# Issuing GpSimd's stores from ScalarE in an attention-plus-MLP backward kernel

## The chip, the cores and the metric

The kernel runs on one core of a Trainium2 chip. Its time is the device time of one execution in microseconds (us). A core has five engines with an instruction queue each: TensorE (PE, matmuls), VectorE (DVE), ScalarE (ACT), GpSimd (Pool) and SyncE (SP, which here only starts transfers). Transfers (DMAs) are started by an instruction in one of these queues and then carried by 16 DMA engines that all queues share. An engine takes its instructions in the order of its queue; where one waits, those behind it wait too.

## The reference

One decoding step of a transformer layer, with the gradients of everything. The inputs are one row x of 640 numbers, the caches K and V (32 heads of 8192 rows by 128), the weights wq, wo, w1, w3, w2, and the gradient of the output.

```python
xn  = layernorm(x)
q   = xn @ wq                                   # 32 heads of 128
p   = softmax(q . K * 128**-0.5)                # per head, over 8192 rows
out = x + (p @ V) @ wo + (silu(xn @ w1) * (xn @ w3)) @ w2
# outputs: out, and by the vjp of grad_out: dx, dK, dV, dwq, dwo, dw1, dw3, dw2
```

For a head, with do the gradient that comes back through wo: dV = p (outer) do; dp = V . do; ds = p * (dp - sum(p * dp)); dK = ds (outer) q; dq = ds @ K. All large arrays are bf16. Each of K, V, dK and dV is 2 MB a head, so a head reads 4 MB and writes 4 MB, and 303.69 MB move in all.

## The kernel before

**A head.** The 8192 rows of a head lie as 128 partitions by 64 rows. K and V of a head are loaded whole by SP (`load_k` L109 into 3 buffers, `load_v` L115 into 2). The products with q and do are made in two halves: VectorE multiplies (`T`, L347, 4 a head) and TensorE adds up the product's columns in PSUM by eight matmuls with the identity (L349, into `psS` for K and `psDP` for V). Then come small steps: the row maximum (`mrow` L382, a matmul to spread it L384, `negM` L389), the exponentials with their sum on ScalarE (`E`, `rsum`, L392), that sum over all partitions on TensorE (L393, called RSUM in what follows), its reciprocal `rZ` on VectorE (L397), the probabilities (`P2` L399, `Pf` on ScalarE L401), `row_dots` (L414 to L418, rdot on TensorE), `U` (L422), and two sets of 64 narrow matmuls that give the head's output and dq (L407, called PV, and L429, called UK).

**The outer products.** dV and dK of a head are made in two halves each, in one of 4 buffers `ot`: in each half ScalarE makes 8 of 32 rows (L362), VectorE the other 24 (L369). When the second half is made, the 2 MB tile is stored by an issue on Pool (L376, 60 tiles). The last two heads are stored in halves by SP (L374).

**The loop.** The loop over heads (L631 to L679) is pipelined by hand: while head c is finished (probabilities, outer products), the products of head n = c + 1 are made between. The loop calls, in this order: product S of n, first half; `probs`; `outer` dV half 0; `keep_dq` of the head before (L465, ScalarE copies `ps_db`); `row_dots`; `attend` (PV); product S, second half; `outer` dV half 1; `dscores` (`U`, `Uf`, UK); `outer` dK half 0; `keep_wq` (wqT, L439); `row_max` of n; product DP, first half; `outer` dK half 1; `exps` of n (negM, E, RSUM); product DP, second half; `weights` (`odq` L444, `dq_diag` L448, `om` L452, and on TensorE db L450, om L455, dxn L458).

**Groups.** Heads go in groups of four (`GH`). Between the steps, at calls of `gap()`, pieces of two generators are put in. `prep_steps` prepares the next group in the group's third and fourth heads: q of four heads (`ps_q`, L257, five matmuls on the loaded `wq_g`), transposes of wo (`ps_t`, L247, called pst4: four matmuls each, copied to `woT` by ScalarE, L252) and do (`ps_d`, L269, called psd; `do_g` L278). `finish_steps` runs in the first head of the next group, the finish head: the sum `on` (L287, L289), 20 matmuls into `accbank` with `wo_g` (L292, called on20), then ScalarE turns `wo_g` in place into dwo (L301, four rows), stores it with `store()` (L126, on Pool) and makes dwq in place of wq (L308, five rows), which is stored after every second group. Stores marked late are kept in a list and issued in head H - 3.

**The start.** The MLP's gradients are made while the first heads load: dw2 in three parts, stored at L558 and L560, dw1 at L589, dw3 at L600, all issued on Pool.

**What sets the order.** The queues of VectorE, ScalarE, SP and Pool keep the order in which the program is written:

```python
with tc.manual_schedule(engines=ORDERED):
```

TensorE is not in `ORDERED`. The framework's scheduler places its matmuls among each other; only PV's first matmul and some at the start are pinned by `tc.keep_in_program_order`.

Of the kernel before, what the change touches and what calls it, by code (L numbers as in the profile page):

```python
# [16 lines left out]
P = 128  # L17
# [4 lines left out]
def kernel(  # L22
# [22 lines left out]
    nc = tc.nc  # L45
# [4 lines left out]
    F = B_w1.shape[1]  # L50
# [10 lines left out]
    NF, REST = divmod(F, P)  # L61
# [31 lines left out]
    dw1_v = out_6.rearrange("(p ci) f -> p ci f", ci=NC)  # L93
    dw3_v = out_7.rearrange("(p ci) f -> p ci f", ci=NC)
    w2_v = B_w2[0:NF * P, :].rearrange("(b p) c -> p b c", p=P)
    dw2_v = out_8[0:NF * P, :].rearrange("(b p) c -> p b c", p=P)

    with tc.manual_schedule(engines=ORDERED):
# [14 lines left out]
        def load_v(h):  # L113
            Vt = (kpool if h == 1 else vpool).tile([P, J, DH], BF16, name="Vt", tag="K" if h == 1 else "V")
            nc.sync.dma_start(Vt[:], vc[h])  # L115
            kv_tiles[h] = kv_tiles.get(h, [None, None])
            kv_tiles[h][1] = Vt
# [4 lines left out]
        def store(dst, src, later=False):  # L122
            if later:
                late.append((dst, src))
            else:
                nc.gpsimd.dma_start(dst, src)  # L126


        def load_wq(b):
# [12 lines left out]
        w1t = kpool.tile([P, NC, F], BF16, name="w1t", tag="K")  # L142
        w3t = kpool.tile([P, NC, F], BF16, name="w3t", tag="K")
        nc.sync.dma_start(w1t[:], w1_v)
        w2_parts = []
        for b0 in range(0, NB, 6):
            nb = min(6, NB - b0)
            nfull = min(nb, NF - b0)
            w2c = opool.tile([P, nb, D], BF16, name="w2c", tag="o")
# [183 lines left out]
        def product(st, which, half):  # L333
            if which == "S":
                st.q = st.G["qs"][:, st.hh, :]
                src, vec = st.K, st.q
            else:
                st.do = st.G["do"][:, st.hh, :]
                src, vec = st.V, st.do
            if half == 0:  # L340
                st.ps = getattr(st, "ps", {})
                st.ps[which] = ps_acc.tile([P, J, RUN], F32, name="ps" + which, tag="acc")
            ps = st.ps[which]
            DHH = DH // 2
            ds_ = slice(half * DHH, (half + 1) * DHH)
            T = tpool.tile([P, J, DHH], BF16, name="T", tag="T")
            nc.vector.tensor_tensor(T[:], src[:, :, ds_], vec[:, ds_].unsqueeze(1).to_broadcast([P, J, DHH]), ALU.mult)  # L347
            for i in range(DHH // RUN):
                nc.tensor.matmul(ps[:], lhsT=ident_bf[:], rhs=T[:, :, RUN * i:RUN * (i + 1)],  # L349
                                 start=(half == 0 and i == 0), stop=(half == 1 and i == DHH // RUN - 1))  # L350

        def outer(st, vec, w2, wf, dst, h, half):
            outer_v(st, vec, w2, dst, h, half, outer_s(st, vec, wf, half))

        def outer_s(st, vec, wf, half):
            if half == 0:
                st.ot = opool.tile([P, J, DH // 2, 2], BF16, name="ot", tag="o")
            j1 = (half + 1) * JH
            if wf is None:
                return j1  # L360
            for j in range(ACT_J):
                nc.scalar.activation(st.ot[:, j1 - ACT_J + j].rearrange("p a b -> p (a b)"), vec, ACTF.Copy,  # L362
                                     scale=wf[:, half, j:j + 1])
            return j1 - ACT_J

        def outer_v(st, vec, w2, dst, h, half, j1):
            j0 = half * JH
            n = j1 - j0
            nc.vector.tensor_tensor(st.ot[:, j0:j1],  # L369
                                    vec.rearrange("p (a b) -> p a b", b=2).unsqueeze(1).to_broadcast([P, n, DH // 2, 2]),  # L370
                                    w2[:, j0:j1, :].unsqueeze(2).to_broadcast([P, n, DH // 2, 2]), ALU.mult)
            rows = st.ot[:].rearrange("p j a b -> p j (a b)")
            if h >= H - TAIL:
                nc.sync.dma_start(dst[h][:, j0:j0 + JH, :], rows[:, j0:j0 + JH, :])  # L374
            elif half:
                nc.gpsimd.dma_start(dst[h], rows)  # L376

        def row_max(st):
            st.S = small.tile([P, J], F32, name="S_sb", bufs=1)
# [7 lines left out]
        def exps(st):  # L387
            negM = small.tile([P, 1], F32, name="negM")
            nc.vector.tensor_reduce(negM[:], st.sm[:, 8:8 + P], AX.X, ALU.max, negate=True)  # L389
            st.E = small.tile([P, J], F32, name="E", bufs=1)  # L390
            rsum = small.tile([P, 1], F32, name="rsum")
            nc.scalar.activation(st.E[:], st.S[:], ACTF.Exp, bias=negM[:], scale=1.0, accum_out=rsum[:])  # L392
            nc.tensor.matmul(st.sm[:, 3:4], lhsT=ones_f, rhs=rsum[:], start=True, stop=True, skip_group_check=True)  # L393
# [26 lines left out]
        def dscores(st):  # L420
            st.U2 = small.tile([P, J, 2], BF16, name="U2", bufs=1)
            nc.vector.scalar_tensor_tensor(st.U2[:], st.DP[:].unsqueeze(2).to_broadcast([P, J, 2]), st.sm[:, 4:5], st.P2[:],  # L422
                                           ALU.subtract, ALU.mult)
            st.Uf = None
            if st.h < H - 1:
                st.Uf = small.tile([P, 2, ACT_J], F32, name="Uf")
                nc.vector.tensor_copy(st.Uf[:], st.U2[:, :, 0].rearrange("p (a j) -> p a j", a=2)[:, :, JH - ACT_J:JH])  # L427
            for j in range(J):
                nc.tensor.matmul(st.ob[:, 1:2], lhsT=st.K[:, j, :], rhs=st.U2[:, j, 0:1], start=(j == 0), stop=(j == J - 1),  # L429
                                 skip_group_check=True)  # L430
# [39 lines left out]
        def mlp_steps():  # L470
# [55 lines left out]
            for wi in range(2):  # L526
# [4 lines left out]
                for k, b0 in enumerate(range(0, NB, 4)):  # L531
# [6 lines left out]
                    src = bc_ps[:].rearrange("p b a -> p (b a)")[:, 0:cols]  # L538
# [10 lines left out]
            def w2_grad(k):  # L549
                b0, nb, nfull, w2c = w2_parts[k]  # L550
                for b, rows in blocks[b0:b0 + nb]:
                    for ci in range(NC):
                        nc.tensor.matmul(accbank[:, OUT0 + ci:OUT0 + ci + 1], lhsT=w2c[0:rows, b - b0, ci * P:(ci + 1) * P],
                                         rhs=hcol_bf[0:rows, b:b + 1], start=False, stop=True, skip_group_check=True)
                    nc.scalar.activation(w2c[0:rows, b - b0, :], g_bc_bf[0:rows, :], ACTF.Copy, scale=hcol[0:rows, b:b + 1])
                    if b in (1, 3, 5, 7, 9):
                        yield
                nc.gpsimd.dma_start(dw2_v[:, b0:b0 + nfull, :], w2c[:, 0:nfull, :])  # L558
                if nfull < nb:
                    nc.gpsimd.dma_start(out_8[NF * P:F, :], w2c[0:REST, nfull, :])  # L560

            dx_ps = ps_w.tile([P, NC, DR1], F32, name="dx_ps", tag="w")

# [22 lines left out]
            grad_v(0, w1t, 0, 2)  # L586
            dx_part(0, w1t, 4, 1)
            grad_v(0, w1t, 2, 3)
            nc.gpsimd.dma_start(dw1_v, w1t[:])  # L589
            load_v(1)  # L590
            yield from w2_grad(1)
            dx_part(1, w3t, 0, 2)
# [4 lines left out]
            grad_s(1, w3t, 0, 4)  # L597
            yield
            grad_v(1, w3t, 4, 1)
            nc.gpsimd.dma_start(dw3_v, w3t[:])  # L600
            load_k(2)
            yield
            nc.vector.tensor_reduce(dxn_mlp[:], dx_ps[:], AX.X, ALU.add)
# [27 lines left out]
        for h in range(H - 1):  # L631
            n = new_head(h + 1) if h + 1 < H else None
            c = hs.pop(h)
            g, hh = divmod(h, GH)
            if n:
                product(n, "S", 0)
            probs(c)
            outer(c, c.do, c.P2, c.Pf, dvc, h, 0)
            if prev:
                keep_dq(prev)  # L640
            gap()
            row_dots(c)
            attend(c)
            turn_wq(c)
            if n:
                product(n, "S", 1)
            outer(c, c.do, c.P2, c.Pf, dvc, h, 1)
            if h + 2 < H:
                load_v(h + 2)
            gap()  # L650
            dscores(c)
            outer(c, c.q, c.U2, c.Uf, dkc, h, 0)
            keep_wq(c)
            if n:
                row_max(n)
                product(n, "DP", 0)
            outer(c, c.q, c.U2, c.Uf, dkc, h, 1)
            if h + 3 < H:
                load_k(h + 3)
            if h == H - 3:  # L660
                for dst, src in late:
                    store(dst, src)
            gap()
            if n:
                exps(n)
                product(n, "DP", 1)
            weights(c)
            gap()
            if hh == 0 and g + 1 < NG:
                if (g + 1) % HB == 0 and g + 1 > HB:  # L670
                    load_wq((g + 1) // HB)
                if g:
                    load_wo(g + 1)
            if hh == 1 and g + 1 < NG:
                steps.append(prep_steps(g + 1))
                gap()
            if hh == 2:
                gap()
            prev = c  # L679
# [85 lines left out]
```

## Time and profile before

| what | us |
| --- | --- |
| time, median of 3 runs (737.46 to 739.82) | 738.92 |
| span of the profiled execution, first to last instruction | 739.3 |
| VectorE busy | 627.9 |
| TensorE busy | 550.8 |
| ScalarE busy | 469.0 |
| Pool busy | 45.7 |

The profile gives one execution. Its span is 0.4 us above the median of the runs. Instructions are grouped by line and by the tiles that they write and read, `out<-in`; "idle before" is the time that the engine stood still just ahead of them, with what ended it. A view of waits sums that time by engine and releaser. The page cuts the span into 40 slices of 18.5 us and gives the busy share of each engine in tenths. Mean durations that the steps use: T 2.28 us, a VectorE outer product of 24 rows 1.75, a ScalarE row 0.389, eight psS matmuls at full TensorE clock 1.89, a store of 2 MB 19.4 us from its issue to its landing, a load of K 25.4. The mean granted TensorE clock is 0.771.

Of the 303.69 MB, 160.39 MB went by the queue of the hardware's descriptors (SP's transfers), 142.30 MB by the software queue (Pool's).

### The profile page before, as it was taken

What the parts mean: (1) busy time and instruction counts of PE and PEld (TensorE: products, weight loads), DVE (VectorE), ACT (ScalarE), POOL (GpSimd) and SP (SyncE); (2) the same over time, 40 slices, a digit from 0 to 9 for tenths busy, and PEclk for the clock granted to TensorE, in tenths of its full rate; (3) what the DMA queues carried; (4) which work ended last, traced back from release to release, by engine and by line L of the source; (5) the groups of instructions that cost most, each with busy time, mean ns of one, the idle gap of its engine ahead of it and who ended that gap; (6) DMA issues with size and microseconds to landing.
All of it is one profiled execution on the core that took longest, in us unless ns stands there. A gap on an engine that the chain in (4) does not pass through costs nothing.

```text
span 739.3 us, 15756 instructions
## 1 busy us (share of the span) xinstructions
PE 550.8 (75%) x6497; PEld 323.2 (44%) x6513; DVE 627.9 (85%) x708; ACT 469.0 (63%) x1395; POOL 45.7 (6%) x87
## 2 busy tenths in 40 slices
PE   4777787777778888685488976788188888789671
PEld 3454444434435454343255444445055444445340
DVE  3689999989699997998389996999469998899992
ACT  2394567686567774694366964686167866668552
POOL 0010000000000100000000100000000000000100
PEclk9697888777976787658696698867687678866875
DMA  9999999999999999999999999999989999999995
GB/s 325 418 396 318 402 430 429 430 425 430 428 432 427 426 430 429 427 431 424 396 402 424 426 431 426 426 433 422 429 341 418 427 425 434 426 430 425 418 413 204
DMA packets 28390, 303.69 MB, mean 411 GB/s; under 512 B 2861, under 2 KB 4591, under 8 KB 10911
## 3 DMA queue, kind: packets, MB, share of 16 engines
q1 hardware_dynamic: 16514, 160.39, 52.3%
q0 software_dynamic: 11792, 142.30, 45.7%
q8 instruction: 51, 0.84, 0.4%
q14 instruction: 21, 0.16, 0.1%
q10 hardware_dynamic: 12, 0.00, 0.0%
HBM read 151.34 MB, written 151.34 MB: 409 GB/s over the span
## 4 chain that ended last, share of the span: by engine, by line
DMA 59%; DVE 23%; PE 13%; SPq 2%; issue 1%; ACT 1%; DVEq 0%; ACTq 0%
DMA Kt<-in_A_k_cache_dram 30%; DMA out_dram<-wo_g 12%; DVE T L347 11%; DMA wq_g<-in_A_wq_dram 8%; DVE ot L369 8%; PE psS L349 5%; DMA out_dram<-ot 5%; DMA wo_g<-in_A_wo_dram 4%; PE ob L407 2%; PE ob L429 1%; DVE DP_sb L414 1%; DVE S_sb L380 1%; PE dx_ps L569 1%; SPq L152 1%; PE ps_t L247 1%
## 5 line engine op out<-in xcount | busy, mean ns | idle before, releaser
L349 PE MATMUL psDP<-T,ident_bf 128*128 128x512 bf16 x512 | 184.6, 523 | 64.8 <-DVE T L347 64.8
L349 PEld LDWEIGHTS <-ident_bf 128*128 128x128 bf16 x1024 | 121.0, 121 | 233.3 <-issue 178.8
L362 ACT ACTIVATE ot<-qs_g,Uf 128x128 bf16<-128x128 bf16 x496 | 151.5, 389 | 34.4 <-DVE Uf L427 26.4
L347 DVE TENSOR_TENSOR T<-Kt,qs_g 128x4096 bf16<-128x4096 bf16 x64 | 146.4, 2289 | 21.7 <-DMA Kt<-in_A_k_cache_dram 20.5
L349 PE MATMUL psS<-T,ident_bf 128*128 128x512 bf16 x512 | 146.5, 438 | 19.0 <-DVE T L347 18.9
L362 ACT ACTIVATE ot<-do_g,Pf 128x128 bf16<-128x128 bf16 x504 | 153.9, 389 | 1.0
L347 DVE TENSOR_TENSOR T<-Vt,do_g 128x4096 bf16<-128x4096 bf16 x64 | 145.9, 2280 | 8.8 <-DMA Vt<-in_A_v_cache_dram 8.8
L369 DVE TENSOR_TENSOR ot<-qs_g,U 128x3072 bf16<-128x3072 bf16 (+1 forms) x64 | 113.1, 1768 | 6.1 <-DMA out_dram<-ot 6.1
L369 DVE TENSOR_TENSOR ot<-do_g,P 128x3072 bf16<-128x3072 bf16 (+1 forms) x64 | 112.8, 1762 | 1.1
L376 POOL DMA_DIRECT2D out_dram<-ot x60 | 32.0, 533 | 584.3 <-DVE Uf L427 247.3
L429 PEld LDWEIGHTS <-Kt 128*128 128x128 bf16 x2048 | 58.8, 100 | 12.6 <-issue 10.9
L429 PE MATMUL ob<-U,Kt 128*128 128x1 bf16 x2048 | 58.0, 164 | 1.6 <-DVE U L422 1.5
L407 PEld LDWEIGHTS <-Vt 128*128 128x128 bf16 x2048 | 57.3, 98 | 0.0
L407 PE MATMUL ob<-P,Vt 128*128 128x1 bf16 x2048 | 57.2, 163 | 0.0
L401 ACT ACTIVATE Pf<-E,rZ 128x16 f32<-128x16 f32 x32 | 9.8, 307 | 57.4 <-DVE rZ L397 57.3
L448 ACT ACTIVATE dq_diag<-ident_bf,odq 128x128 bf16<-128x128 bf16 x32 | 12.8, 399 | 47.7 <-DVE odq L444 47.7
L392 ACT ACTIVATE E<-S_sb,negM 128x64 f32<-128x64 f32 x32 | 11.0, 345 | 41.5 <-DVE negM L389 41.5
L422 DVE SCALAR_TENSOR_TENSOR U<-DP_sb,sm,P 128x128 bf16<-128x128 f32 x32 | 11.1, 348 | 27.3 <-PE sm L418 27.3
L257 PE MATMUL ps_q<-wq_g,xn_col_bf 128*128 128x512 bf16 x32 | 11.3, 469 | 30.4 <-DMA wq_g<-in_A_wq_dram 29.4
L384 PE MATMUL sm<-ident_f,mrow 128*128 128x128 f32 x64 | 19.6, 399 | 16.9 <-DVE mrow L382 16.4
L252 ACT COPY woT<-ps_t 128x512 bf16<-128x512 bf16 x40 | 22.9, 573 | 14.2 <-PE ps_t L247 14.2
L393 PEld LDWEIGHTS sm<-rsum,ones_fc 128*128 128x128 f32 x64 | 18.2, 298 | 19.4 <-ACT E L392 12.0
(151 smaller groups left out, 508.3 us busy)
## 6 DMA issues: line engine op xcount, KB each, us to landing
out_dram<-ot POOLq DMA_DIRECT2D x60, 2048.0 KB, 19.4
Kt<-in_A_k_cache_dram SPq DMA_DIRECT2D x32, 2048.0 KB, 25.4
Vt<-in_A_v_cache_dram SPq DMA_DIRECT2D x32, 2048.0 KB, 21.4
out_dram<-ot SPq DMA_DIRECT2D x8, 1024.0 KB, 12.1
wq_g<-in_A_wq_dram SPq DMA_DIRECT2D x4, 1280.0 KB, 35.1
wo_g<-in_A_wo_dram SPq DMA_DIRECT2D x8, 640.0 KB, 10.9
out_dram<-wo_g POOLq DMA_DIRECT2D x7, 640.0 KB, 21.3
out_dram<-wq_g POOLq DMA_DIRECT2D x3, 1280.0 KB, 30.9
```

The lines of the kernel that those rows point to most:

```text
L252: nc.scalar.copy(woT[:], ps_t[:])
L257: nc.tensor.matmul(ps_q[:], lhsT=xn_col_bf[:, ci:ci + 1].to_broadcast([P, P]), rhs=wq_g[:, ci, :], start=(ci == 0), stop=(ci == NC - 1))
L347: nc.vector.tensor_tensor(T[:], src[:, :, ds_], vec[:, ds_].unsqueeze(1).to_broadcast([P, J, DHH]), ALU.mult)
L349: nc.tensor.matmul(ps[:], lhsT=ident_bf[:], rhs=T[:, :, RUN * i:RUN * (i + 1)], start=(half == 0 and i == 0), stop=(half == 1 and i == DHH ...
L362: nc.scalar.activation(st.ot[:, j1 - ACT_J + j].rearrange("p a b -> p (a b)"), vec, ACTF.Copy, scale=wf[:, half, j:j + 1])
L369: nc.vector.tensor_tensor(st.ot[:, j0:j1], vec.rearrange("p (a b) -> p a b", b=2).unsqueeze(1).to_broadcast([P, n, DH // 2, 2]), w2[:, j0: ...
L376: nc.gpsimd.dma_start(dst[h], rows)
L384: nc.tensor.matmul(st.sm[:, 8:8 + P], lhsT=mrow[:].to_broadcast([P, P]), rhs=ident_f[:], start=True, stop=True, skip_group_check=True)
L393: nc.tensor.matmul(st.sm[:, 3:4], lhsT=ones_f, rhs=rsum[:], start=True, stop=True, skip_group_check=True)
L407: mm = nc.tensor.matmul(st.ob[:, 0:1], lhsT=st.V[:, j, :], rhs=st.P2[:, j, 0:1], start=(j == 0), stop=(j == J - 1), skip_group_check=True)
L429: nc.tensor.matmul(st.ob[:, 1:2], lhsT=st.K[:, j, :], rhs=st.U2[:, j, 0:1], start=(j == 0), stop=(j == J - 1), skip_group_check=True)
L448: nc.scalar.activation(dq_diag[:], ident_bf[:], ACTF.Copy, scale=odq[:, 1:2])
```

## The change

Every DMA that Pool issued is issued by ScalarE: 79 of them. The stores by `store()`, dw2, dw1 and dw3 keep their place in the program. The 2 MB tiles of dV and dK are no longer issued where the second half is made, but put in a list, which is emptied at two places of the loop: after `dscores(c)` (the dV tile) and after `exps(n)` (the dK tile). The last two heads stay on SP. Pool keeps only its constants.

```diff
@@ store()
-                nc.gpsimd.dma_start(dst, src)
+                nc.scalar.dma_start(dst, src)
@@ outer_v()
             elif half:
-                nc.gpsimd.dma_start(dst[h], rows)
+                made.append((dst[h], rows))
+
+        made = []
+
+        def store_made():
+            while made:
+                nc.scalar.dma_start(*made.pop(0))
@@ w2_grad(), and alike for dw1 and dw3
-                nc.gpsimd.dma_start(dw2_v[:, b0:b0 + nfull, :], w2c[:, 0:nfull, :])
+                nc.scalar.dma_start(dw2_v[:, b0:b0 + nfull, :], w2c[:, 0:nfull, :])
@@ the loop over heads
             dscores(c)
+            store_made()
             outer(c, c.q, c.U2, c.Uf, dkc, h, 0)
...
                 exps(n)
+                store_made()
                 product(n, "DP", 1)
```

More of the change, by code (lines that the diff above doesn't have):

```diff
@@ L557, in w2_grad @@
                         yield
-                nc.gpsimd.dma_start(dw2_v[:, b0:b0 + nfull, :], w2c[:, 0:nfull, :])
+                nc.scalar.dma_start(dw2_v[:, b0:b0 + nfull, :], w2c[:, 0:nfull, :])
                 if nfull < nb:
-                    nc.gpsimd.dma_start(out_8[NF * P:F, :], w2c[0:REST, nfull, :])
+                    nc.scalar.dma_start(out_8[NF * P:F, :], w2c[0:REST, nfull, :])
             dx_ps = ps_w.tile([P, NC, DR1], F32, name="dx_ps", tag="w")
@@ L588, in mlp_steps @@
             grad_v(0, w1t, 2, 3)
-            nc.gpsimd.dma_start(dw1_v, w1t[:])
+            nc.scalar.dma_start(dw1_v, w1t[:])
             load_v(1)
@@ L599, in mlp_steps @@
             grad_v(1, w3t, 4, 1)
-            nc.gpsimd.dma_start(dw3_v, w3t[:])
+            nc.scalar.dma_start(dw3_v, w3t[:])
             load_k(2)
```

## The prediction

> **What bounds the kernel now.** I read the slices first, then the chain of waits, then VectorE's waits, then single heads in the timeline. From the page:
>
> ```profile
> PE 550.8 (75%) x6497; PEld 323.2 (44%) x6513; DVE 627.9 (85%) x708; ACT 469.0 (63%) x1395; POOL 45.7 (6%) x87
> DMA  9999999999999999999999999999989999999995
> GB/s 325 418 396 318 402 430 429 430 425 430 428 432 427 426 430 429 427 431 424 396 402 424 426 431 426 426 433 422 429 341 418 427 425 434 426 430 425 418 413 204
> DMA 59%; DVE 23%; PE 13%; SPq 2%; issue 1%; ACT 1%; DVEq 0%; ACTq 0%
> ```
>
> The DMA engines are full in nearly every slice, at 425 to 434 GB/s, and the chain of waits is mostly DMA: the transfers set the pace, about 21 us a head. VectorE (DVE) is close behind. Its waits, and ScalarE's (ACT) on it (us in total, times, longest):
>
> ```profile
> DVE U L422 <- PE sm L418: 27.3, 2, 14.8
> DVE T L347 <- DMA Kt<-in_A_k_cache_dram: 20.5, 13, 3.3
> DVE T L347 <- DMA Vt<-in_A_v_cache_dram: 8.8, 3, 3.8
> DVE ot L369 <- DMA out_dram<-ot: 6.1, 3, 3.0
> ...
> ACT Pf L401 <- DVE rZ L397: 57.3, 28, 4.7
> ```
>
> The first row is DMA too: TensorE (PE) stands in line 257 for `wq_g` (its row: 29.4 us idle for that load), so the rdot sum behind it is late. That makes 62.7 us of DMA waits on VectorE. From one reciprocal rZ (L397, once a head) to the next it takes 18.73 us in heads without a wait (18.9 where a group is finished); from the first at 63.54 us to the last at 712.0 it takes 648.5 us, 30 heads of 21.07 and a shorter last one of 16.5. So VectorE has only **21.07 - 18.77 = 2.3 us a head** to give before it, and not the DMA, sets the pace. This is the number to keep in mind.
>
> One head without a wait that finishes a group (columns: start, us, engine, line):
>
> ```profile
> 482.22 1.89 PE L349 MATMUL psS<-T,ident_bf 128*128 128x512 bf16 x8
> 485.59 0.59 PE L407 MATMUL ob<-P,Vt 128*128 128x1 bf16 x18
> 486.04 0.66 PE L292 MATMUL accbank<-on_bf,wo_g 128*128 128x1 bf16 x20
> 487.79 3.57 PE L349 MATMUL psS<-T,ident_bf 128*128 128x512 bf16 x8
> ```
>
> ```profile
> 479.87 2.29 DVE L347 TENSOR_TENSOR T<-Kt,qs_g 128x4096 bf16<-128x4096 bf16 x1
> 482.08 0.16 DVE L397 RECIPROCAL rZ<-sm 128x1 f32<-128x1 f32 x1
> 485.21 2.29 DVE L347 TENSOR_TENSOR T<-Kt,qs_g 128x4096 bf16<-128x4096 bf16 x1
> ...
> 498.80 2.29 DVE L347 TENSOR_TENSOR T<-Kt,qs_g 128x4096 bf16<-128x4096 bf16 x1
> 501.01 0.16 DVE L397 RECIPROCAL rZ<-sm 128x1 f32<-128x1 f32 x1
> ```
>
> ```profile
> 485.03 0.24 ACT L465 CAST dqbc_g<-ps_db 128x128 bf16<-128x128 f32 x1
> ...
> 486.34 1.55 ACT L301 ACTIVATE wo_g<-g_bc_bf,on 128x640 bf16<-128x640 bf16 x2 [0.79 <-PE accbank L292]
> ...
> 498.67 0.34 ACT L392 ACTIVATE E<-S_sb,negM 128x64 f32<-128x64 f32 x1
> ```
>
> To see: rZ starts 0.09 us before the end of the product T (498.80 + 2.29) and so waits for nothing; the eight psS matmuls of that T end 1.95 us after it (482.22 + 1.89 against 479.87 + 2.29); and ScalarE runs without idle time from 486.34 to E.
>
> **The change, part by part.** *Removed:* 79 DMA issues on Pool, off the path (the Pool rows give 0.53 us each). *Added on ScalarE:* 79 issues. No row prices a store issued there; the nearest are SP's K and V loads at 0.33 us and Pool's slowest at 0.98. I take 0.33. Two or three fall in a head, against ScalarE's waits for VectorE: the Pf row above, 47.7 us in 26 waits before dq_diag and 41.5 in 25 before E, some 5 us a head, so in most heads they are covered; uncovered, 79 x 0.33 = 26 us.
>
> *Moved, and not in the diff:* VectorE's and SP's orders are the same in both built programs, but TensorE's order is set by the framework's scheduler, and with the issues ahead of it on ScalarE it comes out otherwise (S are psS, DP psDP matmuls, PV line 407, UK line 429, on line 292; the number says how many):
>
> ```
> finish head, before: RSUM DP8 db om dxn5 wqT5 S8 | rdot PV18 on20 PV46 S8 UK64
> finish head, after:  DP8 S8 RSUM | rdot PV64 S6 db om dxn5 wqT5 S2 UK64 on20
> group's 3rd, after:  DP8 S8 RSUM | rdot PV64 S6 db om dxn5 wqT5 ps_q5 pst4 S2 UK64 pst4
> group's 4th, after:  DP8 S8 pst4 psd RSUM | rdot PV64 S6 db om dxn5 S2 pst4 psd UK38 psd wqT5 UK26
> ```
>
> (The bar is rZ.) RSUM, the sum of exponentials that rZ reads (L393), now stands **behind the next head's first eight psS**, which wait for T. The step before rZ, hidden until now under DP and T, comes onto VectorE's chain in every head. Likewise db (read by ScalarE's L465) goes behind six psS of the second half, and on20 behind UK. Taking rZ as 0 and start-to-start times from heads without a wait:
>
> - *Ordinary heads (9).* T ends at 18.82; psS ends 1.95 later; RSUM's pair takes 0.35 (the rdot and RSUM rows are 0.25 to 0.4 each at full clock). rZ at **21.1**, +2.4.
> - *Third heads with preparation (7).* The second-half T ends at 5.42. Then S6 (1.42), db to wqT (0.76), ps_q5 (5 x 0.38), pst4 (0.3), S2 (0.47): 10.3. S_sb, at 9.14 in an ordinary head, waits 1.2. T ends at 20.0, S8 at 21.95, pst4 and psd 0.7, RSUM 0.35: **23.0**.
> - *Fourth heads (7).* ScalarE has woT to copy ahead of Pf, and that pst4 now stands behind S2: 5.42 + 1.42 + 0.45 + 0.47 + 0.3 = 8.05. From there woT 0.55, Pf 0.35, 16 rows and L465 (4.9), do_g 1.28, an issue 0.33, 16 rows and wqT (5.25): E at 20.7, its sum 0.5 later, RSUM: **21.6**.
> - *Finish heads (7).* S2 ends at 8.1, UK64 (1.75) at 9.85, and L301 starts 0.3 after on20 does (486.34 against 486.04): 10.15, against 4.26 before. From L301 to E the trace has 12.33 us without idle time (486.34 to 498.67), plus two issues: E at 23.15, RSUM 0.5 later and 0.35 long: **24.0**.
> - *The last:* 16.5 + 2.4 = 18.9.
>
> Sum: 9 x 21.1 + 7 x (23.0 + 21.6 + 24.0) + 18.9 = 689, against 648.5: **+40.5 us**. Four heads come to 89.7 us against 84.3 that the DMA needs, so DMA waits mostly go; the chain is late instead.
>
> *Terms with bounds.* (1) TensorE's clock: these use the full-clock 1.89 us for S8, but the second S8 of a finish head is 3.57 in the row above, and S8 averages 2.27. If the paths see that in finish and fourth heads, +1.7 and +1.0 each, and some first halves: 0 to 24; I take 8, nearer to the first halves' rows, nearly all 1.89. (2) DMA waits that remain, of the 62.7: 0 to 27 (the two `wq_g` waits); `wq_g` landed 41.9 us after its issue and would now be wanted some 40 after: 4. (3) SP's loads and ScalarE's stores now share eight completion semaphores in turn, so a store's issue waits for the transfer eight back. With the trace's landing times that would hold eight stores for 0.8 to 6.5 us, 28 in all; with slack on ScalarE in ordinary heads, 3. (4) The start: dV0 was issued on Pool at 71.19 us, with no packet on its queue before 75.6, while a K load issued by SP at 69.32 had some within 1 us (packet records); -0.8, between 0 and -4.
>
> **Sum:** 739.3 (span of the profiled execution) + 40.5 + 8 + 4 + 3 - 0.8 = 794. The span is 0.4 above the median 738.92, so **793.6 us**.
>
> A rule of the Trainium skill speaks for the change: by "SBUF — State Buffer", section "SBUF: two separate sides", VectorE operations that take the port shared with GpSimd keep Pool-issued DMAs from getting descriptors, and a DMA that ScalarE or SP issues is free of that. The late dV0 agrees with it; the 425 to 434 GB/s with Pool issuing nearly half of the bytes do not show starved engines. By it alone the sum would be rival 1's.
>
> **Rivals.**
>
> *1. The stores leave earlier and the new wait is covered: faster, 732.* Place: the start (-0.8) and the tail, where one DMA engine runs some 6 us after the others by the packet records (slice 40: 204 GB/s): 739.3 - 0.8 - 6. It decides if TensorE's order adds less than 2.3 us to the mean head, for then the DMA still sets the pace. For it: slices 1 to 4 and 40 are below the rest. Against it: the shortest case above is already 2.4. It holds too if ScalarE's issues are simply hidden, as the change means. If a DMA-bound kernel gains nothing at the tail either, the time is 738, no change.
>
> *2. Only RSUM's wait counts: 755.* ScalarE's later db, on and woT might be absorbed. Then the heads are 18.77 + 2.4 = 21.2, level with the DMA's 21.07, and what bunches (SP's 25.9 us waits for a dwo store) still shows: 30 x 0.1 + some 13 of waits left. Against it: ScalarE has no idle time in a finish head to absorb six.
>
> *3. ScalarE is held as well: 835.* The 28 us of shared semaphores fall where ScalarE is on the path, and the clock term is at its 24.
>
> **How the numbers follow.** Forecast 0.66 (775 to 822), rival 2 0.15, rival 3 0.09, rival 1 0.10 (0.07 faster, 0.03 no change). The low end takes in rival 2 with 3 us to spare, the high end the clock and the DMA term nearly whole: 752 to 824, which holds the first two cases. A measurement of this kernel can tell about 0.3% from no change. Faster 0.07, within 0.3% 0.03, slower 0.90.
>
> **What would show it.** In the profile after: VectorE waiting for `sm` of L393's matmul ahead of rZ, about 2 us in each head, where it had none; the chain of waits moving from DMA to VectorE and TensorE; DMA slices below 9 and a mean near 382 GB/s (411 x 739.3 / 794); ScalarE waiting for ps_db (L465) and accbank (L292), 3 to 4 us each time; Pool's row at its constants alone. Wrong if rZ has no wait ahead of it, or the period of ordinary heads stays under 20 us without DMA waits.

## The result and the profile after

The changed kernel takes 843.34 us (median of 4 runs, 838.3 to 844.94) against 739.37 in the same session: a ratio of 1.139, 95% interval 1.135 to 1.143. That is slower, as forecast, but by 104 us instead of 55, and outside the range of 752 to 824.

First the page of the changed kernel, the same lines as before:

```profile
PE 556.8 (66%) x6490; PEld 325.3 (39%) x6513; DVE 631.6 (75%) x708; ACT 467.9 (56%) x1395; POOL 1.7 (0%) x9
DMA  9999999799997999979997999989999799997897
GB/s 335 417 406 351 373 425 387 299 382 373 345 363 300 395 409 365 373 272 431 381 371 300 378 414 372 354 310 389 427 370 364 290 358 381 336 364 295 340 381 276
DVE 49%; PE 30%; ACT 13%; issue 3%; DMA 2%; SPq 1%; ACTq 1%; DVEq 0%
```

VectorE, TensorE and ScalarE are each busy within 6 us of before (only Pool's 45.7 us fall to 1.7), and the span is 101 us longer, so the time is in waits. The transfers no longer set the pace: their share of the chain fell from 59% to 2%, and their rate dips about every fifth slice (299, 300, 272 GB/s), once in a group of four heads. VectorE, TensorE and ScalarE now hand the chain to each other. The waits of the changed kernel (us in total, times, longest):

```profile
ACT dqbc_g L471 <- PE ps_db L456: 114.9, 24, 5.3
...
DVE rZ L403 <- PE sm L399: 104.0, 32, 8.1
...
ACT woT L252 <- PE ps_t L247: 85.0, 16, 10.2
...
DVE T L347 <- ACT do_g L278: 44.6, 7, 6.5
...
DVE S_sb L386 <- PE psS L349: 24.3, 31, 2.6
```

(L399 is L393 of the kernel before: RSUM. L471 is L465, L403 is L397.) VectorE's waits for K, V and `ot`, 35 us before, and the 27 us behind `wq_g` are gone. In their place rZ waits in all 32 heads, and in 7 heads the V product waits for `do_g`. One fourth head of a group, VectorE and then ScalarE:

```profile
536.52 0.22 DVE L388 TENSOR_REDUCE mrow<-S_sb 128x1 f32<-128x64 f32 x1
543.04 2.29 DVE L347 TENSOR_TENSOR T<-Vt,do_g 128x4096 bf16<-128x4096 bf16 x1 [6.30 <-ACT do_g L278]
...
549.58 2.29 DVE L347 TENSOR_TENSOR T<-Kt,qs_g 128x4096 bf16<-128x4096 bf16 x1
553.97 0.17 DVE L403 RECIPROCAL rZ<-sm 128x1 f32<-128x1 f32 x1 [2.09 <-PE sm L399]
```

```profile
536.07 0.59 ACT L252 COPY woT<-ps_t 128x512 bf16<-128x512 bf16 x1 [9.62 <-PE ps_t L247]
536.55 0.31 ACT L407 ACTIVATE Pf<-E,rZ 128x16 f32<-128x16 f32 x1
...
541.73 1.27 ACT L278 CAST do_g<-ps_d 128x512 bf16<-128x512 f32 x1
```

To see: the last T of the head ends at 551.87 and rZ starts 2.1 us later; before, it started 0.09 us ahead of T's end. And ScalarE stood 9.62 us for the transposes that TensorE now makes behind S2; Pf, the rows and do_g follow from there, so VectorE gets do_g 6.30 us late.

From rZ to rZ, the kinds of heads take:

| head | before, no DMA wait | forecast | measured |
| --- | --- | --- | --- |
| ordinary (9) | 18.7 | 21.1 | 19.6 to 22.8, mostly 21.4 to 22.0 |
| third, with preparation (7) | 18.8 (run 1) | 23.0 | 22.7 to 24.1 |
| fourth (7) | 18.7 | 21.6 | 27.8 to 28.4 |
| finish (7) | 18.9 | 24.0 | 25.1 to 27.5 |

No third head of the kernel before is free of waits; 18.8 is from the first run below, which has such heads.

### The profile page after: what moved, and what is told of

Its sections match the earlier page's. It is cut to its first block, busy times and chain, and to the rows that moved or that the text cites. A ratio compares the mean times of both kernels' runs of the same rounds, so it can differ in the third digit from the quotient of the medians.

```text
span 840.5 us, 15689 instructions
## 1 busy us (share of the span) xinstructions
PE 556.8 (66%) x6490; PEld 325.3 (39%) x6513; DVE 631.6 (75%) x708; ACT 467.9 (56%) x1395; POOL 1.7 (0%) x9
## 2 busy tenths in 40 slices
DMA packets 31606, 303.69 MB, mean 361 GB/s; under 512 B 2861, under 2 KB 7599, under 8 KB 14127
## 4 chain that ended last, share of the span: by engine, by line
DVE 49%; PE 30%; ACT 13%; issue 3%; DMA 2%; SPq 1%; ACTq 1%; DVEq 0%
DVE T L347 25%; PE psS L349 17%; DVE ot L369 13%; ACT ot L362 9%; PE ob L413 4%; DVE S_sb L386 2%; DVE DP_sb L420 2%; DMA wq_g<-in_A_wq_dram 2%; PE sm L424 1%; ACT wq_g L308 1%; PE ps_q L257 1%; DVE P L405 1%; ACT do_g L278 1%; ACTq L382 1%; DVE junk L423 1%
## 5 line engine op out<-in xcount | busy, mean ns | idle before, releaser
L349 PE MATMUL psDP<-T,ident_bf 128*128 128x512 bf16 x512 | 163.8, 475 | 99.5 <-DVE T L347 99.5
L349 PEld LDWEIGHTS <-ident_bf 128*128 128x128 bf16 x1024 | 114.3, 114 | 285.4 <-issue 232.4
L349 PE MATMUL psS<-T,ident_bf 128*128 128x512 bf16 x512 | 171.3, 481 | 20.1 <-DVE T L347 19.7
L362 ACT ACTIVATE ot<-qs_g,Uf 128x128 bf16<-128x128 bf16 x496 | 151.4, 390 | 17.2 <-issue 10.1
L424 PE MATMUL sm<-rdot,ones_fc 128*128 128x1 f32 x64 | 16.7, 330 | 102.9 <-DVE junk L423 102.9
L403 DVE RECIPROCAL rZ<-sm 128x1 f32<-128x1 f32 x32 | 5.4, 169 | 104.0 <-PE sm L399 104.0
L471 ACT CAST dqbc_g<-ps_db 128x128 bf16<-128x128 f32 x32 | 8.3, 260 | 114.9 <-PE ps_db L456 114.9
L424 PEld LDWEIGHTS sm<-rdot,ones_fc 128*128 128x128 f32 x64 | 14.0, 272 | 106.1 <-DVE junk L423 106.1
L386 DVE TENSOR_REDUCE S_sb<-psS 128x64 f32<-128x512 f32 x32 | 22.1, 691 | 24.3 <-PE psS L349 24.3
L399 PE MATMUL sm<-rsum,ones_fc 128*128 128x1 f32 x64 | 10.6, 234 | 32.0 <-ACT E L398 32.0
L301 ACT ACTIVATE wo_g<-g_bc_bf,on 128x640 bf16<-128x640 bf16 x28 | 21.6, 817 | 16.2 <-PE accbank L292 16.2
## 6 DMA issues: line engine op xcount, KB each, us to landing
out_dram<-ot ACTq DMA_DIRECT2D x60, 2048.0 KB, 11.5
Kt<-in_A_k_cache_dram SPq DMA_DIRECT2D x32, 2048.0 KB, 12.1
out_dram<-wq_g ACTq DMA_DIRECT2D x3, 1280.0 KB, 12.1
```

What stands on the lines that cost most here:

```text
L301: nc.scalar.activation(wo_g[:, r, :], g_bc_bf[:], ACTF.Copy, scale=on[:, r:r + 1])
L386: nc.vector.tensor_reduce(st.S[:], st.ps["S"][:], AX.X, ALU.add)
L424: nc.tensor.matmul(st.sm[:, 4:5], lhsT=ones_f, rhs=rdot[:], start=True, stop=True, skip_group_check=True)
```

## Experiments

TensorE's order could be taken apart from the queue that issues the stores: at the end of the kernel each matmul is chained behind the one that precedes it in a given list, by an edge that orders issue and waits for nothing.

```python
seq = [pe[a + k] for a, n in PE_ORDER for k in range(n)]
for a, b in zip(seq, seq[1:]):
    tc.add_manual_dep(b, a.name, mybir.DependencyInfo(mybir.DependencyClass.NoSync,
                      mybir.DependencyReason.DATA), reason="order")
```

The runs differ in the list, and in who issues the stores. With the list of the kernel before on the kernel before, the built program is the same instruction for instruction, so the edges themselves cost nothing. Ratios are against the kernel before in the same session (739.4 to 740.2 us). The theories were: **A**, the loss is TensorE's order; **B**, the issues on ScalarE and the shared semaphores cost it.

**1. All stores on ScalarE, TensorE as before.** Edit: the changed kernel with the list of the kernel before.

> The changed kernel, with all stores on ScalarE, but TensorE's matmuls pinned one by one to the order that they had in the kernel before. Theory A (the whole loss is TensorE's new order): the time of before within 1.5%, 730 to 745 us, rZ again without a wait ahead of it, do_g in time. Rival B (the issues on ScalarE and the shared completion semaphores cost the time themselves): still over 790 us, with ScalarE waiting for transfers ahead of E. Between 750 and 790 both have a part.

Measured: 744.91 us, ratio 1.0075 (1.006 to 1.0091). Nearly all of the 104 us is gone and rZ waits for nothing but 0.6 us in one head, with every store still on ScalarE. With TensorE's order of before, theory B has at most 5.5 us. The kernel's waits for DMA are back, and one is new, ScalarE's behind a dwq store:

```profile
DVE U L428 <- PE sm L424: 26.5, 2, 13.5
DVE ot L369 <- DMA out_dram<-ot: 26.4, 3, 9.3
...
ACT dq_diag L454 <- DMA out_dram<-wq_g: 17.1, 2, 9.5
```

**2. All stores on Pool, TensorE as in the changed kernel.** Edit: the kernel before with the other list.

> The kernel before, with all stores on Pool, but TensorE's matmuls pinned to the order that they have in the changed kernel. Theory A: as slow as the changed kernel, 830 to 855 us, with the same waits: some 104 us ahead of rZ, 45 us of the V product for do_g. Rival B: 739 us, no change, since Pool still issues.

Measured: 838.87 us, ratio 1.1353 (1.1334 to 1.1373), whose interval overlaps the changed kernel's (1.1354 to 1.1434). Pool issues, and still:

```profile
DVE rZ L397 <- PE sm L393: 91.0, 32, 5.5
...
DVE T L347 <- ACT do_g L278: 45.3, 7, 6.5
```

So the order makes the loss without the move, and the move without the order makes almost none. Theory A is shown from both sides.

**3. RSUM alone late.** Edit in the list of the kernel before: `DP8 RSUM DP8 ... S8` becomes `DP16 ... S8 RSUM`; stores on Pool.

> The kernel before with one edit to TensorE's order: RSUM stands behind the next head's first eight psS matmuls, everything else as before. Theory A with its parts as measured (2.1 to 2.5 us ahead of rZ a head): four heads take 75.1 + 4 x 2.4 = 84.7 us, level with the 84.3 us of their transfers, so 745 to 770 us. If each head simply gets 2.4 us longer and no DMA wait goes: 739 + 74 = 813. Rival B: 739.

Measured: 772.84 us, ratio 1.045 (1.0413 to 1.0486), 3 us over the range. Its row says why:

```profile
DVE rZ L397 <- PE sm L393: 95.6, 31, 3.8
```

A mean of 3.1 us a head, not 2.4: at the end of ordinary and finish heads rZ waits 3.7. The matmuls ahead of S8 are slow there. In one such head T ends at 440.32 and rZ starts at 444.00:

```profile
437.90 3.50 PE L349 MATMUL psDP<-T,ident_bf 128*128 128x512 bf16 x8 [0.99 <-DVE T L347]
...
441.96 1.89 PE L349 MATMUL psS<-T,ident_bf 128*128 128x512 bf16 x8
```

The second half of DP takes 3.50 us instead of 1.89, and db, om, dxn and wqT follow it; so S8 starts 1.64 us after T's end, and itself takes its 1.89. The mean granted clock of this run is 0.732, against 0.771 before.

**4. Everything late but RSUM.** Edit in the list of the changed kernel: RSUM goes back between the DP halves; stores on Pool.

> The kernel before with TensorE's order as in the changed kernel, except that RSUM stands where it stood before, between the two halves of DP. Theory A: what is left are the late db, on20 and preparation steps: the changed kernel's 843 less 2.1 to 2.5 us in the 23 heads where RSUM alone held rZ, 785 to 800 us; the V product still waits some 6 us for do_g once a group. If RSUM were the main cost, it would be under 760.

Measured: 786.66 us, ratio 1.0634 (1.0604 to 1.0664), as theory A has it. RSUM was the visible row, but the late db, on20 and preparation cost more alone (47 us) than RSUM alone (33).

```profile
DVE T L347 <- ACT do_g L278: 43.9, 7, 6.3
...
DVE rZ L397 <- PE sm L393: 39.9, 14, 5.4
```

Here rZ waits 5.4 us in each of the seven finish heads, where ScalarE is late with E. The two parts add up to 81 us, not to the 104 of the whole order.

**5 and 6. Half of the move, TensorE as before.** Edit of 5: only `made`'s tiles are issued on ScalarE. Edit of 6: only the weight gradients are.

> Only the dK and dV tiles are issued on ScalarE; the weight gradients stay on Pool; TensorE's order pinned to that of before. This asks for the last 5.5 us of the loss (745 against 739 with all stores on ScalarE). Theory C: they come from both kinds sharing the eight completion semaphores: the dwq store, 40 us from issue to landing, holds one, and the dK store eight transfers later waits for it on ScalarE (17.1 us in two waits), after which VectorE waits 9 us for a free ot buffer. Without the weight stores on that queue: 735 to 740 us, no such wait. Rival D (the tiles' issues on ScalarE cost it): 742 to 746.

> Only the weight gradients are issued on ScalarE; the dK and dV tiles stay on Pool; TensorE's order pinned to that of before. Theory C: the dwq store's semaphore is then shared with SP's loads alone, which come round to it later than it lands: 737 to 742 us. Rival (the weight stores' smaller packets or their issues cost it by themselves, at the start and in the tail): 742 to 747.

Measured: 746.07 (ratio 1.0083, 1.0059 to 1.0108) and 745.72 (1.0087, 1.0063 to 1.0111). Theory C falls: in run 5 ScalarE's wait behind the dwq store is gone and the time is not better. Each half alone costs what both cost together. VectorE's waits for DMA (K, V, `ot` and U behind `wq_g`) are only placed otherwise: 62 us in run 5 and 59 in run 6, against 63 before and 64 in run 1.

**7. The changed kernel with a few pins.** Edit:

```diff
+                if i == 0 and (which, half) in (("DP", 1), ("S", 0)):
+                    tc.keep_in_program_order(mm)
...
+            tc.keep_in_program_order(mm)        # and so db, om, dxn, rdot
```

> The changed kernel, with all stores on ScalarE, and instead of a pinned list of all matmuls only some first matmuls kept in program order: of the second DP half (behind RSUM), of the first S half, db, om, dxn and rdot. RSUM then stands between the DP halves again and db ahead of S; on20 stands ahead of rdot in finish heads. Theory A: this is enough, 740 to 752 us. If the exact order elsewhere (preparation, wqT) matters as much: over 765.

Measured: 744.95 us, ratio 1.0073 (1.0048 to 1.0098): the same as with all 6382 matmuls pinned.

**8. The changed kernel, preparation early in fourth heads.** Edit in its list, seven times: `RSUM rdot PV64 S6 db om dxn5 S2 pst4 psd UK38 psd` becomes `RSUM db om dxn5 pst4 psd rdot PV64 S8 psd UK38`.

> The changed kernel's own TensorE order with one edit in the seven fourth heads of a group: db, om, dxn and the last two preparation steps (pst, psd) stand right behind RSUM, ahead of rdot. RSUM stays late everywhere. This tests the term that the prediction lacked: VectorE's V product waited 44.6 us in 7 heads for do_g, which ScalarE makes late. Theory A: that wait goes, 843 - 44 = 795 to 805 us. If something else is late in those heads just behind it, 820 to 843.

Measured: 799.64 us, ratio 1.0817 (1.0788 to 1.0846): 43.7 us less than the changed kernel, and the row has shrunk by 39.3:

```profile
DVE rZ L403 <- PE sm L399: 102.6, 32, 7.8
...
DVE T L347 <- ACT do_g L278: 5.3, 7, 0.8
```

**9. And finish heads early too.** One more edit, seven times: `RSUM rdot PV64 S6 db om dxn5 wqT5 S2 UK64 on20` becomes `RSUM db om dxn5 wqT5 rdot PV18 on20 PV46 S8 UK64`.

> The run before this one (800 us: the changed kernel, with db, om, dxn and two preparation steps early in fourth heads) with one more edit, in the seven finish heads: db, om, dxn and wqT stand right behind RSUM, and on20 inside PV, as in the kernel before. RSUM stays late everywhere. Theory A: ScalarE gets to E some 6 us earlier there, RSUM no longer waits for E, and a finish head falls from some 26.5 us to about 21.5: 800 - 7 x 5 = 760 to 770 us. What is then left over the kernel before is RSUM's wait and the third heads. If the finish heads stay long for another reason: over 785.

Measured: 768.54 us, ratio 1.0381 (1.0361 to 1.0402), 31.1 less. Finish heads take 21.4 us, and rZ waits

```profile
DVE rZ L403 <- PE sm L399: 69.4, 32, 2.9
```

2.2 us in the mean, near the 2.4 that the prediction gave to RSUM alone.

**10. Twice the issues.** Edit, with TensorE as before: `made.extend(...)` with two halves of 1 MB for each tile.

> All stores on ScalarE with TensorE's order pinned to that of before (745 us), and each dK and dV tile stored by two DMAs of 1 MB: 60 more issues on ScalarE at 0.34 us each, 20 us, and shared semaphores that come round sooner. The cover: ScalarE waits some 5 us a head. Theory A: covered, 742 to 750. Rival (issues and semaphore waits on ScalarE are on the path): 755 to 770.

Measured: 742.63 us, ratio 1.0041 (1.0024 to 1.0058), not slower than with 60 issues fewer. But the cover that was expected does not hold. ScalarE now stands some 60 us in ten waits for transfers, and in seven heads, six of them finish heads, rZ waits for RSUM, which waits for E:

```profile
DVE rZ L403 <- PE sm L399: 43.1, 7, 9.7
...
ACT ot L362 <- DMA out_dram<-ot: 21.8, 4, 11.7
```

So issues that wait do reach VectorE here. The time is the same because they take the place of other waits: VectorE's for K and V are gone, and those of U and `ot` fall from 53 us in run 1 to 16, while the DMA engines stay full (411 GB/s).

**11 and 12. An earlier load of `wq_g`.** Edit: `load_wq` one head earlier; 11 with the stores on ScalarE, 12 on Pool, TensorE as before in both.

> All stores on ScalarE, TensorE's order pinned to that of before, and the two later loads of wq_g issued one head earlier. In heads 14 and 22 TensorE waits 12 to 14 us for wq_g while the transfers of the next heads run dry. Expected: those two waits go; as the transfers bound the kernel, only the dips in the transfer rate come back, about 6 us: 737 to 742, against 745 without the edit. If the dips have another reason: 745.

> The kernel before, with stores on Pool, and the same earlier loads of wq_g. Expected by the same reasoning: 732 to 737 us against 739. Against the run with the stores on ScalarE this shows whether a difference of some 5 us stays between the two queues when the waits for wq_g are gone.

Measured: 745.53 (ratio 1.0066, 1.0045 to 1.0087) and 741.13 (1.0018, 1.0003 to 1.0032). The wait behind `wq_g` goes in both, and nothing is gained: both forecasts missed. Between the two queues 4.4 us stay. In run 12 VectorE waits elsewhere instead:

```profile
DVE T L347 <- DMA Vt<-in_A_v_cache_dram: 32.3, 5, 13.2
DVE T L347 <- DMA Kt<-in_A_k_cache_dram: 29.5, 21, 3.3
```

The transfers bound this kernel, and moving a load only moves the wait. No version beats the kernel before.

## Why the prediction was wrong in size

Its cause was right: TensorE's new order, not the move of the issues, takes the time, the DMA stops being the bound, and the sign follows. Steps down from the changed kernel, each one measured (runs of different sessions, in which the kernel before differs by up to 0.8 us):

| from | to | us | what it undoes |
| --- | --- | --- | --- |
| 843.3 (changed) | 799.6 (run 8) | -43.7 | preparation late in fourth heads |
| 799.6 | 768.5 (run 9) | -31.1 | db and on20 late in finish heads |
| 768.5 | 744.9 (run 1) | -23.6 | RSUM late everywhere; db and preparation late in ordinary and third heads |
| 744.9 | 739.4 (before) | -5.5 | the move itself |

- **The step that failed: fourth heads, forecast 21.6, measured 27.8.** The prediction followed ScalarE from woT to do_g and on to E, and asked only when E would be late for RSUM. It put do_g at 13.85 + 1.28, about 15 us after rZ, and did not ask who else reads do_g: the next head's V product, which stands at 10 us on VectorE. By the prediction's own numbers that product would have waited 5 us; it waits the 6.3 us of the row, 44 us in seven heads, nearly as much as the whole miss of 50 us. Run 8 takes the wait away, and 43.7 us with it. (From the first rZ to the last the profile has 755 us against 689 forecast: 44 of these 66 in fourth heads, 17 in finish heads, 4 in ordinary ones. The 14 of the other terms and an end that is 7 us shorter than before offset some of it.)
- **Finish heads, forecast 24.0, measured 26.5 in the mean.** The chain was right: rZ waits some 7 us there, for RSUM, which waits for E. Two of its pieces were priced too low, the matmuls and ScalarE's issues. In the head from 553.97 L301 starts 11.35 us after rZ instead of 10.15, since six psS take 2.72 us instead of 1.42 (in all seven finish heads), and the dV store's issue took 1.04 us instead of 0.33 (0.5 to 2.1 in six of the seven). ScalarE's timeline there:

```profile
562.31 0.27 ACT L471 CAST dqbc_g<-ps_db 128x128 bf16<-128x128 f32 x1 [5.30 <-PE ps_db L456]
...
565.32 1.55 ACT L301 ACTIVATE wo_g<-g_bc_bf,on 128x640 bf16<-128x640 bf16 x2 [2.20 <-PE accbank L292]
...
571.11 1.04 ACTq L382 DMA_DIRECT2D out_dram<-ot  x1
```

  Seven heads by 2.5 is some 17 us. The terms set aside for the clock, DMA and semaphores (15) covered most of it. With the same order and Pool issuing (run 2) finish heads take 25.1 in the mean, so the issues on ScalarE may take some 1.4 us of each. That is from one profile of either kernel; third heads are 0.8 longer in run 2, and the times differ by 4.5 us.
- **Ordinary and third heads**, 21.1 and 23.0: 21.6 and 23.0 in the mean. RSUM's wait at their end is mostly 2.1 to 2.5 us.
- **Terms:** DMA waits that remain, 4: hardly any is left, 1.3 us of TensorE for `wq_g`. Shared semaphores, 3 of 28: in the changed kernel no row has ScalarE behind a transfer, but in five finish heads it stands 10.1 us in all behind its own issues. The semaphore event ahead of the issue of 1.04 us took 17 ns, so that one was not held there; what makes these issues long stays open. An issue on ScalarE, 0.33: the trace has 0.34 as the median, and 78 issues were moved, not 79. The start, -0.8: not to be told. The first rZ came at 64.8 instead of 63.5, but 2.1 of that is its wait for RSUM, and in the runs where it waits for nothing it comes anywhere from 62.8 to 65.3.
- **Rival 1**, faster by earlier packets, is excluded with its condition met: in run 1 only the stores' queue and their place in it differ, and it is 0.75% slower. The Trainium skill's rule ("SBUF — State Buffer", section "SBUF: two separate sides") that VectorE operations which take the port shared with GpSimd keep Pool-issued DMAs from their descriptors is not seen here: the tiles land 19.4 us after their issue on Pool and 20.2 on ScalarE in run 1. The Trainium skill also says, in "DMA: Bandwidth & Descriptors", section "Issuing engines are not separate DMA queues", that starting DMAs on several engines saves only the time that a sequencer takes to start them. Run 1 agrees with that: it is not faster.
- **Rival 2** (755, ScalarE absorbs the rest) is not what happened, though RSUM alone on the kernel before cost 33 us (run 3). **Rival 3** came near the size, 835, for the wrong reason: what is missing is the wait for do_g, not held issues.

*Open:* the 5.5 us (0.7%) of the move itself. Each half alone costs as much as the whole (runs 5 and 6), twice the issues cost less (run 10), and theory C fell. In run 1's profile the heads take 648.1 us from the first rZ to the last, as before (648.5); its span is 3.4 us longer, for more time ahead of the first (1.5) and behind the last (2.3). In run 5's the heads take 11.7 us longer and the end 5.5 less. With one profile of each, these runs don't settle where the time goes, or why. Why the scheduler places the matmuls otherwise when ScalarE has these issues is open too.

That the dK and dV tiles set off the new order can be read from the built programs alone: with only the tiles moved TensorE's order is nearly that of the changed kernel, with only the weight gradients it is nearly that of before.

## What to carry to other kernels

Where a framework orders one engine by itself, an edit to another engine's queue can be an edit to that engine too: compare the order of all engines in the built programs before pricing the diff, and pin the few instructions whose place matters. When a step comes late, follow every reader of what it makes, not only the one that leads to the next step already in mind. And a kernel that transfers bound hides some slack per head (2.3 us here); beyond it a microsecond on the chain costs about a microsecond (run 8: 39.3 us of waits less, 43.7 us of time).

## What was not expected of the hardware

- ScalarE's queue starts a transfer while earlier work still runs: in the finish head of the changed kernel the dK store, behind E in program order, is issued at 577.64 us, and E starts at 579.35. Rows of ScalarE's timeline:

```profile
577.64 0.34 ACTq L382 DMA_DIRECT2D out_dram<-ot  x1
578.13 1.32 ACT L308 ACTIVATE wq_g<-dqbc_g,xn_col 128x512 bf16<-128x512 bf16 x2
579.35 0.34 ACT L398 ACTIVATE E<-S_sb,negM 128x64 f32<-128x64 f32 x1
```

- The weight gradients go out in smaller packets from ScalarE's queue than from Pool's: 28389 packets in run 5, where they stay on Pool, and 31605 in run 6, where they alone are moved, for the same 303.69 MB. Their 16.47 MB are 3152 packets on Pool's queue in run 5 and 6380 on ScalarE's in run 6.
- With the chain as the bound, a load of K lands 12.1 us after its issue instead of 25.4, and a tile's store 11.5 instead of 19.4 (12.3 where Pool issues it, in run 2; all medians). So 13 of a load's 25 us and some 7 of a store's 19 were not the transfer alone; that they went into waiting for other transfers fits the full DMA engines before, but was not tested.
